# A recurrent-attention and mixture-of-experts kernel: units 0 to 3 and steps 0 to 13 in a written order, weight conversion cut into single operations

## The chip, the cores and the metric

The kernel runs on one core of one Trainium2 chip. Its time is the device time of one execution in microseconds (us), the median of several. A profile of one further execution gives every instruction's start and end on the engines: PE (TensorE, with its weight loads shown apart as PEld), DVE (VectorE), ACT (ScalarE), POOL (GpSimd) and SP (SyncE, which here only issues DMA transfers).

## What is computed

Three layers follow one another. A recurrent attention over 768 tokens for 2 batches of 8 heads of 48, a dense layer of 384 to 2048 to 384 with an exponential unit, and 8 experts of 384 to 1024 to 384, one chosen per token. The dense layer's weights come as 64-bit floats, the others as 32-bit.

```python
for t in range(S):
    kt, vt, rt = (k[:, :, t], v[:, :, t], r[:, :, t])
    cur = np.einsum('bhd,bhe->bhde', u[None] * kt, vt)
    y[:, :, t] = np.einsum('bhd,bhde->bhe', rt, state + cur)
    state = w[None, :, :, None] * state + np.einsum('bhd,bhe->bhde', kt, vt)
...
h = x @ w_in
g = np.where(h > 0.0, h, alpha * (np.exp(np.minimum(h, 0.0)) - 1.0))
return (g @ w_out).astype(np.float32)
...
expert_idx = np.argmax(logits, axis=1)
h = np.maximum(np.einsum('ecd,edf->ecf', disp, w1), 0.0)
y = np.einsum('ecf,efd->ecd', h, w2)
out[i] = gate_w[i] * y[expert_idx[i], pos[i]]
```

## The kernel before, in words

**Units.** The recurrence is cut into 24 units: a unit is 128 tokens of one batch and four heads. `Unit` has these parts: `decay` (DVE, scales `rk`), `bonus` (two products on `tok`, DVE for units 0 to 7, then POOL), `diagonal` (a sum on DVE, then an affine select on POOL that makes `am`), `scores` (PE into the one bank `a`), `mask` (DVE, reads `a`, completes `am`), `decay_kt` (DVE, `kh`), `out` (PE, into the one bank `y`, from `am` and the state `st`), `state` (PE, into bank `u`), `carry` (ACT or DVE, `u` to `st`), `split_y` (ACT, the high part of `y` in `yh`), `split_y_low` (DVE, the low part), and `pack`, DMAs that lay `yh` into `xT`. Units of the same half of the heads (u, u + 2, ...) hand a state on.

**Steps.** The dense layer runs in 48 steps q. A step multiplies one block of 256 tokens (`xT[g]`, four units) with two blocks of 128 columns: `ff_in` (18 matmuls), then `elu_exp`, `elu_min` (ACT), `elu_max` (DVE), `elu_hi` (ACT), `elu_lo` (DVE in steps 0 to 3, then POOL), and `ff_out(q - 2)` (18 matmuls into banks x0 and x1). Every number is carried as a high and a low part, so each product takes three matmuls. Step 0 needs units 0 to 3, step 4 needs units 4 to 7; steps 0 to 3 hold one whole unit each (`whole`), step 4 and 5 none, later steps half a unit each (`half`).

**Weights.** The 64-bit weights come in 16 pieces of 768 KB, n = 0 to 15 (`SEQ`: pieces 0, 1, 2, 4 of `w_in` and 3, 5, 6, 7 of `w_out` serve steps 0 to 5, the other eight serve steps 8 to 13). A piece goes through a load; a copy of a byte of each number (ACT, `b7`); two bit operations (DVE, `b5`, `b7`); a widening to `f64` (ACT); an OR with the rest of the bits (DVE, `f64<-raw`; a 32-bit float now); the high part (ACT, `w<-f64`); and the low part, which is a difference: for pieces 0, 1, 2, 3 and 5 by PE (identity times `f64` less identity times the high part, then a copy by ACT from bank h), for piece 4 on DVE, for the other ten on POOL (line 230).

**Order.** From step 9 on, the program is written under `manual_schedule`: each engine takes its instructions as written. All before that (units 0 to 3, in steps -8 to -1, and steps 0 to 8) is put in order by a scheduler, from the written one. There, weight conversion is called in portions by the table `FILL`, three stages for a pair of pieces at a time. SP and ACT issue DMAs in their own order, so a DMA that waits for a buffer holds up those behind it.

Of the kernel before, what the change touches and what calls it, by code (L numbers as in the profile page):

```python
# [42 lines left out]

FILL = {-6: (0, 1, 0), -5: (0, 1, 0), -4: (0, 1, 0), -3: (0, 1, 0), -2: (0, 1, 0), -1: (0, 1, 0),
        0: (2, 1, 2), 1: (1, 1, 2), 2: (2, 1, 2), 3: (1, 1, 2), 4: (2, 1, 2), 5: (2, 1, 2), 6: (1, 1, 2), 7: (1, 1, 2),
        8: (1, 1, 2), 9: (1, 1, 0)}
LO_V = (4,)
LO_P = (0, 1, 2, 3, 5)
CARRY_P = range(2, 8)
AUTO = 9  # L50
ELO_V = (0, 1, 2, 3)
BONUS_V = range(8)
INIT = (7, 16)
PACKS = (0, 1, 2, 3, 7)


def rwkv_moe_kernel(tc, rkT, tok, wT, ub, rkvT, wu, w_in, w_out, w_gate, w1, w2, out, cap):
# [113 lines left out]
    def load_f64(n, ahead=True):  # L171


        o, i = SEQ[n]
        src = (w_out if o else w_in)[i // 2, i % 2]
        if 0 < n < 3 and ahead:
            raw = first.tile([P, 768, 2], U32, name=f"raw{n}")
        elif n % 3 == 1:
# [6 lines left out]
    words, side = {}, [att]  # L185

    def bits_f64(n, step, ahead=True):

        raw = raw64[n]
        if step == 0:
            words[n] = side[0].tile([P, 192], U32, tag="b7", name="b7", bufs=2)
            byte = raw.rearrange("p n t -> p (n t)").bitcast(I8).rearrange("p (n t) -> p n t", t=8)[:, :, 4]
            nc.scalar.copy(words[n].bitcast(I8), byte)
        elif step == 1:
            top = words[n]
            t = words[n] = side[0].tile([P, 768], U32, tag="f64", name="f64", bufs=2)
# [5 lines left out]
            nc.scalar.activation(out=t.bitcast(I32), in_=top.bitcast(I8), func=AF.Copy, scale=float(1 << 24))  # L204
        else:
            t = words.pop(n)
            nc.vector.scalar_tensor_tensor(out=t, in0=raw[:, :, 0], scalar=5, in1=t,
                                           op0=ALU.logical_shift_right, op1=ALU.bitwise_or)
            del raw64[n]
            o, i = SEQ[n]  # L210
            dst, pool = (wout_t, wpb) if o else (win_t, [wp])
            if i % 2 == 0:
                if o and not wpb:
                    first.release()
                    wpb.append(tc.alloc_tile_pool(name="wpb", bufs=4, side="left", reuse_waits="tile"))
                dst.append(pool[0].tile([P, 2, 1536], F32R, tag="w", name="w"))
            pending.append((n, dst[i // 2], slice(i % 2 * 768, (i % 2 + 1) * 768), t))
            if not ahead:
                return
            if n == 0:  # L220
                load_f64(5)
            elif 3 <= n < 13:
                load_f64(n + 3)

    def split_bits(n, w, o, t):
        nc.scalar.copy(w[:, 0, o], t.bitcast(F32))
        if n in LO_P:
            two_low.append((w, o, t))
            return
        (nc.vector if n in LO_V else nc.gpsimd).tensor_tensor(  # L230
            out=w[:, 1, o], in0=t.bitcast(F32), in1=w[:, 0, o].bitcast(F32), op=ALU.subtract)

    two_low = []

    def low_bits():

        while two_low:
            w, o, t = two_low.pop(0)
            for a, b in ((0, 512), (512, 768)):
                ps = ps_tile(psH, "h")[:, 0:b - a]  # L240
                group(ps, [(ident, t[:, a:b].bitcast(F32))], stop=False)
                group(ps, [(nident, w[:, 0, o.start + a:o.start + b])], start=False)
                nc.scalar.copy(w[:, 1, o.start + a:o.start + b], ps)  # L243

# [26 lines left out]
    class Unit:  # L271
# [95 lines left out]
        def pack(self):  # L367
# [350 lines left out]
    def prep(u, stage):  # L718
# [58 lines left out]
    def whole(q, n):  # L777

        x = units[n]
        prep(n + 1, 0)  # L780
        while pending:
            split_bits(*pending.pop(0))
        x.scores()
        fill(q, 0)
        prep(n + 1, 2)
        ff_in(q, range(2))
        elu_exp(q)
        elu_min(q)
        x.mask()
        x.out()  # L790
        x.state()
        x.split_y()
        low_bits()
        if q >= LAG:
            ff_out(q - LAG)
        fill(q, 1)
        elu_max(q)
        units.pop(n).split_y_low()
        elu_hi(q)
        finish(q)  # L800
        elu_lo(q)
        x.carry()
        prep(n + 1, 3)
        fill(q, 2)

    def half(q, n, first):

        x = units.get(n)
        ff = 0 <= q < NQ
        if first:  # L810
            prep(n + 1, 0)
        elif not ff:
            prep(n + 1, 2)
        while pending:
            split_bits(*pending.pop(0))
        if not first and ff:
            prep(n + 1, 2)
        fill(q, 0)
        if ff:
            ff_in(q, range(2))  # L820
            elu_exp(q)
            elu_min(q)
        if x and first:
            x.scores()
        elif x:
            x.out()
            x.state()
        low_bits()
        if q - LAG >= 0:
# [3 lines left out]
        elif x:  # L833
            x.split_y()
        fill(q, 1)
        if ff:
# [9 lines left out]
        if x and not first:  # L846
            x.carry()
            prep(n + 1, 3)
        fill(q, 2)

    if True:
        load_unit(2)
        load_f64(0)
        load_unit(3)
        load_f64(1)
        load_unit(4)
        load_f64(2)
        load_unit(5)
        load_f64(3)
        load_f64(4)  # L860
        prep(0, 0)
        prep(0, 2)
        prep(0, 3)
        for q in range(-8, 0):
            half(q, 4 + q // 2, q % 2 == 0)
        for q in range(4):
            whole(q, 4 + q)
        for q in range(4, AUTO):
            half(q, 4 + (q + 2) // 2 if q > 5 else NU, q % 2 == 0)
            if INIT[0] <= q < INIT[0] + 6:  # L870
                init_slots(q - INIT[0])
            elif INIT[1] <= q < INIT[1] + 4:
                init_out(q - INIT[1])
    with tc.manual_schedule():
        for q in range(AUTO, 38):
            half(q, 4 + (q + 2) // 2, q % 2 == 0)
            if INIT[0] <= q < INIT[0] + 6:
# [138 lines left out]
    def again():  # L1016
# [14 lines left out]
        wout_t.clear()  # L1031
        conv[:] = [(n, step) for n in range(16) for step in range(3)]
        load_f64(0, False)
        for n, step in list(conv):
            bits_f64(n, step, False)
            if step == 2:
                x = pending.pop()
                nc.scalar.copy(x[1][:, 0, x[2]], x[3].bitcast(F32))
                sub("v", x[1][:, 1, x[2]], x[3].bitcast(F32), x[1][:, 0, x[2]])
                if n < 15:  # L1040
                    load_f64(n + 1, False)
        conv.clear()
        nc.gpsimd.memset(ohc[0], 0.0)
# [106 lines left out]
```

## Time and profile before

| | us |
|---|---|
| median of 3 runs | 467.74 (467.67 to 471.47) |
| the profiled execution's own time | 469.95 |
| its span, first to last instruction | 468.1 |
| PE busy in the span | 436.8 (93%) |
| DVE, ACT, POOL busy | 256.8, 232.3, 149.0 |

The span is what the views below show. The 1.85 us between span and time lie outside the engines' instructions, and the profiled execution was 2.21 us over the median. Mean granted TensorE clock: 0.974 of full speed.

### The profile page before, as it was taken

What the parts mean: (1) busy time and instruction counts of PE and PEld (TensorE: products, weight loads), DVE (VectorE), ACT (ScalarE), POOL (GpSimd) and SP (SyncE); (2) the same over time, 40 slices, a digit from 0 to 9 for tenths busy, and PEclk for the clock granted to TensorE, in tenths of its full rate; (3) what the DMA queues carried; (4) which work ended last, traced back from release to release, by engine and by line L of the source; (5) the groups of instructions that cost most, each with busy time, mean ns of one, the idle gap of its engine ahead of it and who ended that gap; (6) DMA issues with size and microseconds to landing.
All of it is one profiled execution on the core that took longest, in us unless ns stands there. A gap on an engine that the chain in (4) does not pass through costs nothing. (4 is left out here: it accounts for less than half of the span.)

```text
span 468.1 us, 8885 instructions
## 1 busy us (share of the span) xinstructions
PE 436.8 (93%) x3454; PEld 414.8 (89%) x3454; DVE 256.8 (55%) x500; ACT 232.3 (50%) x382; POOL 149.0 (32%) x173
## 2 busy tenths in 40 slices
PE   1959999989999999999999999998999999999992
PEld 1737878979999999999999999998999999999991
DVE  6665677696337484437443424746755655656410
ACT  3362987867334333433444356644456456455410
POOL 4111135668544545434432332423011011011011
PEclk9987999989999999999999999998999999999997
DMA  8866875634724533131300282342766765763001
GB/s 246 263 216 205 249 257 179 211 100 143 261 67 128 192 120 103 46 97 62 110 21 18 69 321 70 101 154 66 247 203 220 236 214 202 252 225 117 27 29 31
DMA packets 27330, 71.14 MB, mean 152 GB/s; under 512 B 4229, under 2 KB 12732, under 8 KB 27280
## 3 DMA queue, kind: packets, MB, share of 16 engines
q1 hardware_dynamic: 24832, 65.06, 42.4%
q0 software_dynamic: 1792, 4.75, 3.0%
q10 hardware_dynamic: 656, 0.69, 0.5%
q8 instruction: 29, 0.48, 0.5%
q14 instruction: 21, 0.17, 0.1%
HBM read 53.89 MB, written 12.46 MB: 142 GB/s over the span
## 5 line engine op out<-in xcount | busy, mean ns | idle before, releaser
L391 PE MATMUL h<-xT,w 128*128 128x256 f32 x864 | 113.4, 285 | 1.1 <-DMA xT<-yh 1.1
L443 PE MATMUL x<-g,w 128*128 128x256 f32 x864 | 114.0, 286 | 0.2 <-ACT w L243 0.2
L443 PEld LDWEIGHTS x<-g,w 128*128 128x128 f32 x864 | 106.1, 191 | 3.9 <-issue 1.0
L391 PEld LDWEIGHTS h<-xT,w 128*128 128x128 f32 x864 | 106.7, 190 | 2.1 <-DMA xT<-yh 1.3
L413 POOL TENSOR_TENSOR g<-e,g 128x512 fp32r<-128x512 f32 x44 | 57.3, 1302 | 106.2 <-ACT g L410 106.2
L607 DVE TENSOR_TENSOR w<-raw,w 128x1536 fp32r<-128x1536 f32 x32 | 57.1, 1784 | 34.3 <-ACT w L606 33.5
L268 PE MATMUL y<-w,ht 128*112 128x384 f32 (+1 forms) x384 | 73.0, 339 | 0.0
L268 PE MATMUL h<-dT,w 128*128 128x240 f32 x576 | 69.8, 275 | 0.0
L268 PEld LDWEIGHTS h<-dT,w 128*128 128x128 f32 x576 | 68.9, 189 | 0.2 <-ACT dT L645 0.2
L406 DVE SCALAR_TENSOR_TENSOR e<-h,e 128x512 f32<-128x512 f32 x48 | 33.0, 686 | 59.3 <-ACT e L402 59.1
L268 PEld LDWEIGHTS y<-w,ht 128*112 128x112 f32 (+1 forms) x384 | 65.2, 181 | 0.2
L398 ACT ACTIVATE e<-h 128x512 f32<-128x512 f32 x48 | 28.6, 597 | 62.3 <-PE h L391 60.7
L707 POOL DMA_INDIRECT out<-o,ds x16 | 15.5, 966 | 121.5 <-ACT o L705 119.1
L606 ACT CAST w<-raw 128x1536 fp32r<-128x1536 f32 x32 | 47.3, 1477 | 0.0
L677 ACT ACTIVATE ht<-h 128x480 fp32r<-128x480 f32 x32 | 18.3, 572 | 57.5 <-PE h L268 57.0
L410 ACT CAST g<-e 128x512 fp32r<-128x512 f32 x48 | 29.8, 621 | 32.1 <-DVE e L406 30.9
L678 DVE SCALAR_TENSOR_TENSOR ht<-h,ht 128x480 fp32r<-128x480 f32 x32 | 21.0, 656 | 32.9 <-ACT ht L677 32.9
L295 POOL TENSOR_SCALAR_AFFINE_SELECT am<-dt 128x512 f32<-128x512 f32 x24 | 17.7, 737 | 45.3 <-PE y L268 24.3
L402 ACT ACTIVATE e<-e 128x512 f32<-128x512 f32 x48 | 30.3, 632 | 1.3
L318 DVE COPY_PREDICATED am<-maskf,a 128x512 f32<-128x512 int32 x24 | 17.8, 740 | 16.7 <-PE a L268 16.6
L268 PE MATMUL a<-rk 48*128 48x128 f32 x192 | 19.7, 325 | 7.1 <-DVE rk L282 6.2
L268 PEld LDWEIGHTS a<-rk 48*128 48x128 f32 x192 | 14.5, 208 | 11.2 <-DVE rk L282 6.2
(137 smaller groups left out, 458.3 us busy)
## 6 DMA issues: line engine op xcount, KB each, us to landing
raw<-w SPq DMA_DIRECT2D x32, 768.0 KB, 5.9
tok<-tok SPq DMA_DIRECT2D x24, 288.0 KB, 3.4
raw<-w_in SPq DMA_DIRECT2D x8, 767.6 KB, 6.8
raw<-w_out SPq DMA_DIRECT2D x8, 767.6 KB, 4.6
rk<-rkT SPq DMA_DIRECT2D x24, 224.0 KB, 3.1
disp<-zrow SPq DMA_DIRECT2D x6, 776.0 KB, 6.0
out<-zrow SPq DMA_DIRECT2D x4, 576.0 KB, 4.2
xT<-yh SPq DMA_DIRECT2D x22, 96.0 KB, 2.3
```

Of the source, the lines that this page charges most:

```text
L268: nc.tensor.matmul(out, x, y, start=start and n == 0, stop=stop and n == len(pairs) - 1, skip_group_check=True)
L391: nc.tensor.matmul(h_ps[:, j], win(d, f, a), x[:, :, d, c], start=n == 0, stop=n == 8)
L398: nc.scalar.activation(out=e, in_=hps[q], func=AF.Exp)
L402: nc.scalar.activation(out=elu[q], in_=elu[q], func=AF.Relu, bias=1.0, scale=-1.0)
L406: nc.vector.scalar_tensor_tensor(out=e, in0=hps.pop(q), scalar=0.0, in1=e, op0=ALU.max, op1=ALU.subtract)
L410: nc.scalar.copy(gt[q][:, 0], elu[q])
L413: eng("v" if q in ELO_V else "p").tensor_tensor(out=gt[q][:, 1], in0=elu.pop(q), in1=gt[q][:, 0].bitcast(F32), op=ALU.subtract)
L443: nc.tensor.matmul(o, wout(f, d, a), gg[:, c, j], start=pr in x2at[g] and j == 0 and n == 0 and d != 1, stop=pr + 1 in x2at[g] and j == 1 ...
L606: nc.scalar.copy(w[:, 0], raw)
L607: low.tensor_tensor(out=w[:, 1], in0=raw, in1=w[:, 0].bitcast(F32), op=ALU.subtract)
L677: nc.scalar.activation(out=ht[:, 0], in_=h_ps, func=AF.Relu)
L678: nc.vector.scalar_tensor_tensor(out=ht[:, 1], in0=h_ps, scalar=0.0, in1=ht[:, 0].bitcast(F32), op0=ALU.max, op1=ALU.subtract)
```

## The change

The whole program up to the experts now stands under `manual_schedule`. Units 0 to 3 (with parts of unit 4) are written out in `first_units`. Weight conversion is cut into single operations with one letter each: R is the load of a piece, K the byte copy, A the two bit operations, L the widening, B the OR, H the high part, W the low part (for pieces 0 to 3 the matmuls of it, whose copy by ACT is V); U is the load of a unit. The table `PLAN` says which stand at which place (a, b, v, w, d, e, f) of which step up to 12. The low parts of pieces 6 to 15 are now on DVE, of 4 and 5 on POOL, of 0 to 3 on PE (through banks x0 and x1 in place of h). `elu_lo` of steps 0 to 3 comes one step later. Loads of pieces and units stand later among the other transfers, the load of piece 0 ahead of those of units 2 and 3; which packing DMAs ACT issues changes (`PACKS`).

```diff
-FILL = {-6: (0, 1, 0), -5: (0, 1, 0), -4: (0, 1, 0), -3: (0, 1, 0), -2: (0, 1, 0), -1: (0, 1, 0),
...
-LO_V = (4,)
-LO_P = (0, 1, 2, 3, 5)
+PLAN = {0: {"b": "B2 R5", "d": "K4 H2", "e": "B3 R6", "f": "H3 U7"},
+        1: {"b": "A4", "v": "W2", "d": "V2 L4 K5", "w": "W3", "e": "B4 R7", "f": "V3 H4 K6 U8"},
...
+for n in range(8, 16):
+    PLAN[n - 3] = {"b": f"B{n} " + (f"R{n + 3} " if n < 13 else "") + (f"A{n + 1}" if n < 15 else ""),
+                   "d": f"H{n} " + (f"L{n + 1} " if n < 15 else "") + (f"K{n + 2}" if n < 14 else ""), "f": f"W{n}"}
+LO_V = range(6, 16)
+LO_P = range(4)
...
-PACKS = (0, 1, 2, 3, 7)
+PACKS = (3, 7)
...
+        elif n in LO_P and side[0] is att:
+            low_bits(op, n)
...
+            hi, lo = place64(n)
+            (nc.vector if n in LO_V or side[0] is not att else nc.gpsimd).tensor_tensor(
+                out=lo, in0=whole64.pop(n).bitcast(F32), in1=hi.bitcast(F32), op=ALU.subtract)
...
+                ps = low_ps[n, a] = ps_tile(psX, tag)[:, 0:b - a]
...
-                (nc.scalar if self.u in PACKS and n % 2 == 0 else nc.sync).dma_start(
+                (nc.scalar if self.u in PACKS and n % 2 else nc.sync).dma_start(
...
+        x[2].scores()
+        x[1].out()
+        x[1].split_y()
+        do("A0 K1 L0")
+        x[1].state()
+        end(1)
+        do("R3")
+        x[1].carry()
+        x[2].mask()
+        begin(3)
+        x[2].decay_kt()
+        middle(3)
+        x[3].scores()
+        x[2].out()
+        x[2].split_y()
+        do("A1 L1 B0 H0")
...
+    with tc.manual_schedule():
+        do("R0 U2 U3 R1")
+        first_units()
         for q in range(4):
             whole(q, 4 + q)
-        for q in range(4, AUTO):
...
+        for q in range(4, 38):
+            step(q)
```

Three places show what the scheduler had made of the order and what is written now. The first is ACT around the carry of unit 2 (`st_f0`) and the high part of unit 2's y (`yh_299` before, `yh_295` now). Before:

```order
L339 COPY st_f0_150<-u_294 48x2x48 x2
L204 ACTIVATE f64_301<-b7_259 128x768
L226 CAST w_322<-f64_279 128x768
L195 COPY b7_374<-raw2_188 128x768
L243 CAST w_322<-h_341 128x512
L243 CAST w_322<-h_345 128x256
L226 CAST w_322<-f64_301 128x768
L204 ACTIVATE f64_426<-b7_374 128x768
L195 COPY b7_376<-raw_194 128x768
L226 CAST w_452<-f64_426 128x768
L195 COPY b7_518<-raw_196 128x768
L360 CAST yh_299<-y_148 112x2x128
```

On the same engine now:

```order
L225 ACTIVATE f64_260<-b7_216 128x768
L350 COPY st_f1_151<-u_262 48x2x48 x2
L371 CAST yh_295<-y_148 112x2x128
L225 ACTIVATE f64_300<-b7_258 128x768
L231 CAST w_303<-f64_260 128x768
L350 COPY st_f0_150<-u_305 48x2x48 x2
```

Before, unit 2's `yh` stood behind ten rows of conversion that come after the carry; now it stands ahead of the widening of piece 1.

The second place is DVE around the mask of unit 9, in steps 8 and 9 (`e<-h` is `elu_max`, `f64<-raw` the OR of a piece). Before:

```order
L406 SCALAR_TENSOR_TENSOR e_994<-h_975,e_994 128x512
L363 TENSOR_TENSOR yh_1024<-y_148,yh_1024 112x2x128
L207 SCALAR_TENSOR_TENSOR f64_1026<-raw_900,f64_1026 128x768
L200 TENSOR_SCALAR b5_1115<-b7_1060 128x192
L202 SCALAR_TENSOR_TENSOR b7_1060<-b7_1060,b5_1115 128x192
L318 COPY_PREDICATED am_968<-maskf_129,a_1084 128x512
L207 SCALAR_TENSOR_TENSOR f64_1114<-raw_952,f64_1114 128x768
```

Now:

```order
L293 TENSOR_TENSOR rk_751<-rk_751,ew_100 112x512
L228 SCALAR_TENSOR_TENSOR f64_974<-raw_814,f64_974 128x768
L219 TENSOR_SCALAR b5_1032<-b7_976 128x192
L221 SCALAR_TENSOR_TENSOR b7_976<-b7_976,b5_1032 128x192
L329 COPY_PREDICATED am_942<-maskf_129,a_1063 128x512
L417 SCALAR_TENSOR_TENSOR e_1054<-h_1035,e_1054 128x512
L236 TENSOR_TENSOR w_1057<-f64_974,w_1057 128x768
```

One OR, one pair of bit operations and one low part now stand in each step, the low part last.

The third place is POOL from step 4 on (line 230 before and line 236 now are low parts of weights, lines 413 and 424 `elu_lo`). Before:

```order
L230 TENSOR_TENSOR w_755<-f64_732,w_755 128x768
L230 TENSOR_TENSOR w_824<-f64_809,w_824 128x768
L413 TENSOR_TENSOR g_815<-e_788,g_815 128x512
L413 TENSOR_TENSOR g_877<-e_853,g_877 128x512
L230 TENSOR_TENSOR w_824<-f64_818,w_824 128x768
L230 TENSOR_TENSOR w_899<-f64_883,w_899 128x768
L230 TENSOR_TENSOR w_951<-f64_888,w_951 128x768
```

Now:

```order
L236 TENSOR_TENSOR w_460<-f64_616,w_460 128x768
L306 AFFINE_SELECT am_689<-dt_687 128x512
L424 TENSOR_TENSOR g_809<-e_782,g_809 128x512
L424 TENSOR_TENSOR g_866<-e_838,g_866 128x512
L299 TENSOR_TENSOR tok_655<-tok_655,u_bc_93 128x192
L300 TENSOR_TENSOR tok_655<-tok_655 128x192
L424 TENSOR_TENSOR g_936<-e_901,g_936 128x512
```

The low parts of weights are gone from POOL behind piece 5.

## Rows read from the trace of the kernel before

**Rows 1.** Four stretches: length, busy us of each engine, granted clock, DMA share, GB/s.

```profile
0.00:42.20 42.20, 26.26 (x150) 19.72 (x150) 26.73 (x77) 17.81 (x38) 8.76 (x26) 0.88 0.71 227
42.20:73.20 31.00, 29.13 (x209) 24.31 (x207) 21.60 (x42) 23.90 (x45) 9.40 (x12) 1.00 0.81 259
73.20:122.40 49.20, 47.13 (x394) 45.09 (x395) 35.16 (x51) 34.36 (x56) 31.77 (x23) 0.97 0.52 169
122.40:468.00 345.60, 334.23 (x2706) 325.69 (x2704) 173.30 (x332) 156.28 (x244) 99.06 (x113) 0.99 0.40 131
```

**Rows 2.** Waits of PE up to 125 us: for whom, total, times, longest.

```profile
PE y L268 <- DVE yh L363: 4.8, 1, 4.8
...
PE y L268 <- DVE am L318: 2.1, 1, 2.1
```

**Rows 3.** Instructions in order of time, first units: start, length, engine, line.

```profile
5.48 0.68 DVE L282 TENSOR_TENSOR rk<-rk,ew 112x512 f32<-112x512 f32 x1
...
21.82 1.10 PE L268 MATMUL y<-am,tok 128*48 128x128 f32 x8
...
34.42 0.36 ACT L360 CAST yh<-y 112x256 fp32r<-112x256 f32 x1
...
38.26 0.42 DVE L363 TENSOR_TENSOR yh<-y,yh 112x256 fp32r<-112x256 f32 x1 [2.73 <-ACT yh L360]
...
42.21 0.98 PE L391 MATMUL h<-xT,w 128*128 128x256 f32 x6
```

**Rows 4.** Groups by line and shape, DVE, 0 to 43 us: busy, mean ns, idle before.

```profile
L282 DVE TENSOR_TENSOR rk<-rk,ew 112x512 f32<-112x512 f32 x8 | 5.8, 730 | 1.0 <-DMA rk<-rkT 1.0
L318 DVE COPY_PREDICATED am<-maskf,a 128x512 f32<-128x512 int32 x6 | 4.4, 727 | 2.4 <-PE a L268 2.4
L207 DVE SCALAR_TENSOR_TENSOR f<-raw,f 128x768 uint32<-128x768 uint32 x3 | 2.9, 955 | 0.7 <-ACT f L204 0.7
...
L288 DVE TENSOR_TENSOR tok<-tok,u_bc 128x192 f32<-128x192 f32 x7 | 2.5, 354 | 0.5 <-DMA u_bc<-ub 0.5
...
L363 DVE TENSOR_TENSOR yh<-y,yh 112x256 fp32r<-112x256 f32 x5 | 2.1, 424 | 7.4 <-ACT yh L360 7.4
...
L200 DVE TENSOR_SCALAR b<-b 128x192 uint32<-128x192 uint32 x5 | 1.3, 257 | 1.1 <-ACT b L195 1.1
```

**Rows 5.** Instructions in order of time, around step 9 and before step 4.

```profile
66.14 1.05 PE L268 MATMUL h<-f,idwg 128*128 128x512 f32 x2
...
73.19 0.95 PE L391 MATMUL h<-xT,w 128*128 128x256 f32 x6 [1.14 <-DMA xT<-yh]
...
97.20 2.67 POOL L230 TENSOR_TENSOR w<-f,w 128x768 fp32r<-128x768 f32 x1 [2.27 <-ACT w L226]
...
103.13 3.79 PE L443 MATMUL x<-g,w 128*128 128x256 f32 x18
```

**Rows 6.** Groups by line and shape, all engines, 0 to 125 us.

```profile
L230 POOL TENSOR_TENSOR w<-f,w 128x768 fp32r<-128x768 f32 x10 | 19.6, 1965 | 9.7 <-ACT w L226 7.5 <-DMA raw<-w_out 2.2
L207 DVE SCALAR_TENSOR_TENSOR f<-raw,f 128x768 uint32<-128x768 uint32 x16 | 17.4, 1086 | 8.4 <-ACT f L204 8.4
...
L413 POOL TENSOR_TENSOR g<-e,g 128x512 fp32r<-128x512 f32 x9 | 12.1, 1340 | 10.0 <-ACT g L410 10.0
...
L200 DVE TENSOR_SCALAR b<-b 128x192 uint32<-128x192 uint32 x16 | 7.7, 483 | 4.2 <-ACT b L195 4.1
L202 DVE SCALAR_TENSOR_TENSOR b<-b,b 128x192 uint32<-128x192 uint32 x16 | 7.6, 476 | 0.4
...
L230 DVE TENSOR_TENSOR w<-f,w 128x768 fp32r<-128x768 f32 x1 | 1.0, 959 | 0.5 <-ACT w L226 0.5
```

**Rows 7.** Instructions in order of time, PE, the `ff_in` of steps 10 and 12.

```profile
106.75 2.31 PE L391 MATMUL h<-xT,w 128*128 128x256 f32 x18
...
117.32 2.31 PE L391 MATMUL h<-xT,w 128*128 128x256 f32 x18
```

**Rows 8.** The loads of weight pieces up to 60 us, from issue to landing.

```profile
DMA to landing us min/median/max: 4.1/6.4/9.8
```

More of the change, by code (lines that the diff above doesn't have):

```diff
@@ L225, in split_bits @@
[L225 to L243, printed above, removed]
+        elif op == "L":
+            t = whole64[n] = side[0].tile([P, 768], U32, tag="f64", name="f64", bufs=2)
+            nc.scalar.activation(out=t.bitcast(I32), in_=words.pop(n).bitcast(I8), func=AF.Copy, scale=float(1 << 24))
+        elif op == "B":
+            t = whole64[n]
+            nc.vector.scalar_tensor_tensor(out=t, in0=raw64.pop(n)[:, :, 0], scalar=5, in1=t,
+                                           op0=ALU.logical_shift_right, op1=ALU.bitwise_or)
+        elif op == "H":
+            nc.scalar.copy(place64(n)[0], whole64[n].bitcast(F32))
+        elif n in LO_P and side[0] is att:
+            low_bits(op, n)
+        else:
+            hi, lo = place64(n)
+            (nc.vector if n in LO_V or side[0] is not att else nc.gpsimd).tensor_tensor(
+                out=lo, in0=whole64.pop(n).bitcast(F32), in1=hi.bitcast(F32), op=ALU.subtract)
@@ new lines, in rwkv_moe_kernel, with low_bits, do @@
+    low_ps = {}
+    def low_bits(op, n):
+        hi, lo = place64(n)
+        for tag, a, b in (("x0", 0, 512), ("x1", 512, 768)):
+            if op == "W":
+                ps = low_ps[n, a] = ps_tile(psX, tag)[:, 0:b - a]
+                group(ps, [(ident, whole64[n][:, a:b].bitcast(F32))], stop=False)
+                group(ps, [(nident, hi[:, a:b])], start=False)
+            else:
+                nc.scalar.copy(lo[:, a:b], low_ps.pop((n, a)))
+    def do(ops):
+        for x in ops.split():
+            bits_f64(x[0], int(x[1:]))
@@ L779, in whole, with late_lo @@
         x = units[n]
+        plan = PLAN[q]
+        x.scores()
+        x.mask()
         prep(n + 1, 0)
[L781 to L784, printed above, removed]
+        late_lo()
+        do(plan.get("a", ""))
+        ff_in(q, range(2))
         prep(n + 1, 2)
-        ff_in(q, range(2))
+        do(plan.get("b", ""))
         elu_exp(q)
         elu_min(q)
-        x.mask()
+        do(plan.get("v", ""))
         x.out()
+        x.split_y()
         x.state()
-        x.split_y()
-        low_bits()
+        do(plan.get("w", ""))
+        do(plan.get("d", ""))
+        units.pop(n).split_y_low()
         if q >= LAG:
             ff_out(q - LAG)
-        fill(q, 1)
+        x.carry()
         elu_max(q)
-        units.pop(n).split_y_low()
+        prep(n + 1, 3)
+        do(plan.get("e", ""))
         elu_hi(q)
         finish(q)
[L801 to L804, printed above, removed]
+        do(plan.get("f", ""))
+    def late_lo():
+        for q in list(elu):
+            if q in gt:
+                elu_lo(q)
     def half(q, n, first):
@@ L809, in half @@
         ff = 0 <= q < NQ
+        plan = PLAN.get(q, {}) if side[0] is att else {}
+        late_lo()
         if first:
             prep(n + 1, 0)
-        elif not ff:
+        else:
             prep(n + 1, 2)
[L814 to L818, printed above, removed]
+        do(plan.get("b", ""))
         if ff:
@@ L848, in half, with first_units, begin, middle @@
             prep(n + 1, 3)
[L849 to L865, printed above, removed]
+        do(plan.get("f", ""))
+    def first_units():
+        x = [None] * 5
+        def begin(n):
+            x[n] = units[n] = Unit(n)
+            x[n].decay()
+        def middle(n):
+            x[n].bonus()
+            x[n].diagonal()
+        def end(n):
+            units.pop(n)
+            x[n].split_y_low()
+        begin(0)
+        middle(0)
+        x[0].scores()
+        begin(1)
+        x[0].mask()
+        middle(1)
+        x[0].decay_kt()
+        x[1].scores()
+        x[0].out()
+        do("K0")
+        x[0].split_y()
+        begin(2)
+        x[1].mask()
+        x[0].state()
+        end(0)
+        do("U4 R2")
+        x[1].decay_kt()
+        x[0].carry()
+        middle(2)
+        x[2].scores()
[14 more added lines that the diff above has]
+        do("A1 L1 B0 H0")
+        x[2].state()
+        end(2)
+        do("U5")
+        x[2].carry()
+        x[3].mask()
+        begin(4)
+        x[3].decay_kt()
+        do("K2 B1")
+        x[3].out()
+        x[3].split_y()
+        do("H1")
+        x[3].state()
+        end(3)
+        do("R4 U6 W0 V0 K3")
+        x[3].carry()
+        middle(4)
+        x[4].decay_kt()
+        do("A2 W1 V1 L2 A3 L3")
@@ L1031, in again @@
         wout_t.clear()
-        conv[:] = [(n, step) for n in range(16) for step in range(3)]
         load_f64(0, False)
[L1034 to L1042, printed above, removed]
+        for n in range(16):
+            do(f"K{n} A{n} L{n} B{n} H{n} W{n}")
+            if n < 15:
+                load_f64(n + 1, False)
         nc.gpsimd.memset(ohc[0], 0.0)
```

83 lines of the change are left out of this document (30 added, 53 removed), and 3 rows, old and new, of the table PLAN.

## The prediction

> **What bounds the kernel now.** I read the stretches first, because one average hides three regimes. PE is the engine that the end hangs on: from 122.4 us to the end it is busy 334.2 of 345.6 us [rows 1], and the order there is the same in both programs, so whatever the change brings must show as an earlier start of that stretch, which is `ff_in` of step 13. Ahead of it there are three stages. In the first, to 42.2 us (the first `ff_in`), PE is busy 26.3 of 42.2 us, much of it at half speed (granted clock 0.88), so it is a chain that bounds, not PE. In the second, steps 0 to 3, PE is busy 29.1 of 31.0 us: nearly bound. In the third, steps 4 to 12, 47.1 of 49.2 us.
>
> Next, who makes PE wait. The longest wait of an order's making is 4.8 us for unit 2's low part on DVE [rows 2]. The time line says why: the last matmuls of unit 2's y end at 22.9 us, but ACT makes the high part of that y only at 34.42 us [rows 3], 11.5 us later. DVE is not what it waited for; ACT had ten conversion rows in front. The second wait, 2.1 us for a mask [rows 2], is in step 9: there low parts on POOL take up to 2.67 us, and 18 matmuls of `ff_out` take 3.79 us [rows 5] where an undisturbed `ff_in` of 18 takes 2.31 us [rows 7]: after its pause PE ran part of them slower (mean granted clock 0.97 in that stage [rows 1]). The undisturbed pace is that of rows 7: 10.57 us for two steps, 5.28 us each.
>
> **Part 1: units 0 to 3 as written.** The number wanted is when the first `ff_in` can start. DVE has the longest list. From the first `decay`, which starts at 5.48 us [rows 3] and moves little, to unit 3's low part, it now holds 5 `decay` and 4 masks at 0.73, 2 ORs at 0.96, 4 low parts at 0.42, 2 bit operations at 0.26, and 19 small ones (bonus, diagonal, `kh`, the second bit operation, the negated identity) at 0.35 [rows 4] (shapes without a row are taken as the 128x192 one): 6.6 + 1.9 + 1.7 + 0.5 + 6.7 = 17.4 us. Without a wait unit 3's low part ends at 22.9 us; before it ended at 38.7 us [rows 3]. Waits come on top. I followed the rows of the new order by hand, with one bank `a` (scores of a unit behind the mask of the one before), one bank `y` (out behind the low part of the one before) and PE at its slow pace (1.10 us for the y matmuls [rows 3]): DVE waits for unit 1's y, for unit 2's y and a little for unit 3's, about 2.5 us in all. So 25.3 us.
>
> Behind it come the packing DMAs: before, 3.5 us from the end of unit 3's low part to the first matmul of `ff_in` [rows 3]. That gives 28.8 us. But PE has its own list: unit 3's state ends at about 26.2 us, then low parts of pieces 0 and 1, then the scores of unit 4. The two fp32 passes of a 512-wide piece take 1.05 us [rows 5], so a piece of 768 about 1.6 us; half-speed doubles part of it, and piece 1's must wait for ACT's copy out of x0. I take 2.2 us each and 0.7 us for scores: 31.3, say **31.5 us in place of 42.2, a gain of 10.7 us**. The floor is 28.5 us (PE's list hidden behind the packing); with both low parts at half speed and 2 us more of waits it is 35 us.
>
> The loads that are moved: piece 0 now goes ahead of units 2 and 3, 768 KB, which at the 227 GB/s of this stage [rows 1] delays unit 2's by 3.5 us at most. By my walk through the new order unit 2's `decay` is due at about 10.8 us and its scores wait for unit 1's mask until about 12.2 us anyway. This costs 0 to 2 us of the chain; I take 0. Later pieces stand behind packing DMAs on SP; the first copies of pieces 2 and 3 are due on ACT at about 23 and 29 us, 8 and 10 us after their loads can be issued, against 6.4 us to land [rows 8]. Nothing is lost while landing stays under 8 us.
>
> **Part 2: steps 0 to 3.** PE was nearly full here, so only work that leaves helps. Before, four pieces (1, 2, 3, 5) had their low parts made by PE in this stage, now two (2 and 3; piece 1 is done earlier and counted above, piece 5 goes to POOL): 2 x 1.6 = 3.2 us off 31.0, so 27.8. On the other side ACT holds eleven rows in step 1, some 8 us, a little more than PE; and step 4 again waits for the packing of unit 7 (1.1 us before [rows 5]), now with less PE work to cover it. I take 29 us, between 27.5 and 32: **a gain of 2 us**.
>
> **Part 3: steps 4 to 12.** The low parts of ten pieces were on POOL, 1.97 us each; now ten (6 to 15) are on DVE at 0.96 [rows 6]: 9.6 us more for DVE. Against this stands what DVE lost beside POOL: its bit operations took 0.483 and 0.476 us in the mean where they take 0.257 and 0.354 alone, the OR 1.086 against 0.955 [rows 4, 6]: 16 x (0.226 + 0.122 + 0.131) = 7.7 us. So DVE's 35.2 us of this stage [rows 1] become about 37, in 46 us: it fits. ACT's list is the old one. With the masks no longer behind stretched bit operations, the 2.1 us wait and the slow matmuls behind it go; what is late next is PE itself, at the pace of rows 7. Seven steps at 5.28 us are 37.0; steps 4 and 5 have no unit but ACT's `keep_half` in the way, 9 us together: 46 us in place of 49.2, **a gain of 3 us**. Bounds: 44.5 (nothing waits in steps 4 and 5), and 52 for the rival below.
>
> **Sum.** 10.7 + 2 + 3 = 15.7 us. A fixed order cannot take another instruction when one is late; for this I take back 2 us, the idle time that PE had in the third stage [rows 1]. Gain 13.7 us, and step 13 at 108.7 us. The profiled execution would take 469.95 - 13.7 = 456.3 us; it was 2.2 us above the median of 467.74, so the median comes to **454 us**. One per cent, 4.7 us, is about what a measurement of this kernel can tell from no change.
>
> **A rule of the skill that speaks against it.** In rows 6 the operations of DVE grow beside POOL, and POOL's low part grows to 2.67 us [rows 5]. The Trainium skill, "SBUF — State Buffer", "Who interferes with whom", says that a DVE instruction with two SBUF inputs and a GpSimd instruction that reads SBUF exclude each other for the whole instruction. The subtraction moved to DVE is such an instruction, so by that rule it gives no relief against what stays on POOL. The first rival below works this out from rows.
>
> **Rivals.**
> (A) *DVE becomes the bound in steps 4 to 12.* POOL keeps `elu_lo`, 1.34 us a step [rows 6], and half of each later unit's bonus. If DVE stands still for each `elu_lo` and half a microsecond more, its step is 37 / 9 = 4.1 us plus 1.8, 5.9 against PE's 5.28: 0.65 x 9 = 6 us. Time 460. For it: DVE is the engine that got work. Against it: POOL's load falls by 8 low parts, 15.7 us, and what was stretched most stood beside the low parts now gone.
> (B) *The change does not do what it says for the first units:* they stay bound by loads and by PE at half speed, so that only about half of part 1 is got and parts 2 and 3 are eaten by waits. Gain 5 us, 463. For it: DMA share 0.71 in the first stage [rows 1]. Against: ACT held unit 2's y for 11.5 us with the data there.
> (C) *Slower: loads of pieces 9 to 15.* Each load now waits on SP for the OR three pieces earlier, and the copy of its bytes stands on ACT a little over one step, 6.3 us, behind it, ahead of the next `elu_exp`. If loads land after 9.8 us [rows 8], ACT stands still 3.5 us for each of 7 pieces, and PE with it: 24 us, 478 us. It decides from 8.3 us on (7 x 2 us eat the 14). Against: the median is 6.4 us in the stretch with the fullest queues, and this stage's DMA share is 0.52 [rows 1].
> (D) *All of it at the floor:* 28.5, 27.5 and 44.5 us, 100.5 for step 13, a gain of 22 us: 446.
>
> **How the numbers follow.** Forecast 0.58, A 0.18, B 0.10, C 0.06, D 0.08. Faster by over 1% (under 463.1): the forecast, A, D and a third of B, 0.87. Slower by over 1%: C, 0.06. Between: 0.07. The range holds the forecast and A and most of D: from 447 to 462; left out are B, C and the end of D.
>
> **What would show it.** In the changed profile: the first `ff_in` near 31.5 us, with unit 2's `yh` on ACT within 1 us of its matmuls; `ff_in` of step 4 near 60.5 and of step 13 near 108.7 us, with full clock from step 0 on; no mask wait in step 9; DVE's bit operations near 0.26 and 0.35 us; SP loads landing before their copy. Part 1 is wrong if PE waits over 2 us for `xT` at step 0 or DVE for loads of units 2 and 3. A shows as PE waits for DVE in steps 4 to 12, C as ACT waits for `raw`. The whole is wrong if something behind step 13 moves, for example the order of the tail's DMAs, which I take as fixed.

## The result, and the profile of the changed kernel

The changed kernel took 456.19 us in the median of four runs (455.42 to 456.84), the kernel before beside it 468.15 us: a ratio of 0.973 (95% interval 0.968 to 0.978), 12.0 us less. The profiled execution of the changed kernel took 456.53 us with a span of 454.8 us, so the spans, which the views show, differ by 13.3 us.

The stretches of the changed kernel, cut where those of before were cut (first `ff_in`, `ff_in` of step 4, of step 13, end), with the same columns:

```profile
0.00:30.70 30.70, 19.84 (x120) 14.63 (x120) 21.95 (x62) 15.38 (x35) 7.00 (x25) 1.00 0.80 238
30.70:60.00 29.30, 27.39 (x227) 23.59 (x225) 25.98 (x48) 23.29 (x44) 10.17 (x8) 1.00 0.77 238
60.00:109.10 49.10, 46.98 (x400) 44.37 (x401) 41.05 (x64) 35.69 (x57) 22.16 (x18) 1.00 0.67 221
109.10:454.80 345.70, 334.15 (x2706) 325.76 (x2704) 176.11 (x337) 157.68 (x246) 100.59 (x115) 0.99 0.40 133
```

Against [rows 1] the first stretch lost 11.5 us, the second 1.7, the third 0.1 and the last nothing. So most of what the change is worth lies ahead of the first `ff_in`; nine steps in a new order, with ten subtractions moved to another engine, are worth nothing in sum.

The waits of PE up to 125 us (for whom, total, times, longest):

```profile
PE a L279 <- DVE rk L293: 7.4, 2, 6.2
PE x L279 <- ACT w L250: 1.7, 1, 1.7
...
PE x L454 <- ACT half L437: 1.3, 1, 1.3
...
PE x L454 <- POOL w L236: 0.7, 1, 0.7
PE x L454 <- DVE w L236: 0.6, 2, 0.4
```

The 4.8 us for unit 2's low part and the 2.1 us for the mask of step 9 [rows 2] are gone. New are four small waits of `ff_out` (x, line 454), for three writers, and 1.7 us in the first units, where PE's low part of piece 1 waits for ACT to copy that of piece 0 out of x0. The 6.2 us is the start of the program, before the first data.

The chain that bounded the first stretch, instructions in order of time:

```profile
12.07 0.69 DVE L293 TENSOR_TENSOR rk<-rk,ew 112x512 f32<-112x512 f32 x1 [1.13 <-DMA rk<-rkT]
...
20.20 1.10 PE L279 MATMUL y<-am,tok 128*48 128x128 f32 x8
...
21.34 0.37 ACT L371 CAST yh<-y 112x256 fp32r<-112x256 f32 x1 [2.24 <-PE y L279]
...
25.69 0.42 DVE L374 TENSOR_TENSOR yh<-y,yh 112x256 fp32r<-112x256 f32 x1 [1.18 <-ACT yh L371]
...
28.27 1.13 PE L279 MATMUL x<-f,idwg 128*128 128x512 f32 x2 [1.73 <-ACT w L250]
...
30.75 2.42 PE L402 MATMUL h<-xT,w 128*128 128x256 f32 x18
```

Unit 2's y ends at 21.30 and its high part starts 0.04 us later, where 11.5 us lay between them before [rows 3]. The order has turned round: ACT now waits for PE. Unit 3's low part ends at 26.1 us (38.7 before) and the first `ff_in` starts at 30.75, straight behind PE's other work and without a wait in front of it. The first row is a cost of the moved load: DVE waits 1.13 us for the data of unit 2, which now come behind piece 0.

The starts of `ff_in` of steps 4, 9, 10, 11 and 13:

```profile
60.01 2.51 PE L402 MATMUL h<-xT,w 128*128 128x256 f32 x18 [1.24 <-DMA xT<-yh]
...
84.79 2.32 PE L402 MATMUL h<-xT,w 128*128 128x256 f32 x18
90.67 2.32 PE L402 MATMUL h<-xT,w 128*128 128x256 f32 x18
97.11 2.32 PE L402 MATMUL h<-xT,w 128*128 128x256 f32 x18
...
109.13 2.31 PE L402 MATMUL h<-xT,w 128*128 128x256 f32 x18
```

Those of steps 9 and 13 in the kernel before (step 10 is in [rows 7]):

```profile
97.14 2.37 PE L391 MATMUL h<-xT,w 128*128 128x256 f32 x18
...
122.41 0.76 PE L391 MATMUL h<-xT,w 128*128 128x256 f32 x5
```

Step 9 took 9.61 us before and takes 5.88 now: 3.73 gained. Steps 10 to 12 took 15.66 together and now take 18.46: 2.80 lost. Steps 4 to 8 take 0.83 more, but PE is busy in all of them in both kernels; before, part of step 4's `ff_out` stood ahead of the cut. That is the 0.1 us of the third stage: not an unmoved stage, but a gain of which most is given back.

### The profile page after: what moved, and what is told of

Its sections match the earlier page's. It is cut to its first block, busy times and chain, and to the rows that moved or that the text cites. A ratio compares the mean times of both kernels' runs of the same rounds, so it can differ in the third digit from the quotient of the medians.

```text
span 454.8 us, 8861 instructions
## 1 busy us (share of the span) xinstructions
PE 428.4 (94%) x3448; PEld 408.4 (90%) x3448; DVE 265.1 (58%) x509; ACT 232.0 (51%) x380; POOL 139.9 (31%) x165
## 5 line engine op out<-in xcount | busy, mean ns | idle before, releaser
L454 PEld LDWEIGHTS x<-g,w 128*128 128x128 f32 x864 | 104.5, 188 | 6.0 <-ACT half L437 1.5
L424 POOL TENSOR_TENSOR g<-e,g 128x512 fp32r<-128x512 f32 x44 | 58.9, 1338 | 124.4 <-ACT g L421 124.4
```

The lines of the kernel that those rows point to most:

```text
L424: eng("v" if q in ELO_V else "p").tensor_tensor(out=gt[q][:, 1], in0=elu.pop(q), in1=gt[q][:, 0].bitcast(F32), op=ALU.subtract)
L454: nc.tensor.matmul(o, wout(f, d, a), gg[:, c, j], start=pr in x2at[g] and j == 0 and n == 0 and d != 1, stop=pr + 1 in x2at[g] and j == 1 ...
```

## The experiments

Each ratio is to the kernel before in runs on the same chip; the changed kernel's is 0.973 (0.968 to 0.978).

**Unit 2's y behind the conversion again.** In `first_units`:

```diff
         x[2].out()
-        x[2].split_y()
         do("A1 L1 B0 H0")
         x[2].state()
+        x[2].carry()
+        do("K2")
+        x[2].split_y()
         end(2)
         do("U5")
-        x[2].carry()
...
-        do("K2 B1")
+        do("B1")
```

> The changed kernel with one thing moved back: on ACT the high part of unit 2's y stands behind the widening of piece 1, the high part of piece 0 and the byte copy of piece 2 (2.6 us of work), as conversion stood ahead of it before the change. If ACT's order in the first units is what made the first ff_in late (my part 1), the high part comes 2.5 to 3.5 us later and the first ff_in starts 2 to 3.5 us later, at 33 to 34 us in place of 30.7; the time is 458.5 to 460. Rival: PE's own list and the packing hide it (both ended together at 30.7 us); then the first ff_in moves by less than 1 us and the time stays at 456 to 457.

Measured: 458.81 us (457.31 to 460.95), ratio 0.981 (0.977 to 0.985). ACT in order of time, and PE's wait for it, in this kernel:

```profile
24.76 0.86 ACT L215 COPY b<-raw 128x768 int8<-128x768 int8 x1
25.65 0.37 ACT L371 CAST yh<-y 112x256 fp32r<-112x256 f32 x1
```

```profile
PE y L279 <- DVE yh L374: 2.3, 1, 2.3
```

Four ACT rows in front of that one `yh`, against ten in the kernel before: unit 2's y ends at 22.48 us and waits 3.2 us for ACT, and PE waits 2.3 us behind it where it waited 4.8 [rows 2]. The first `ff_in` comes 4.1 us later (34.81) and step 13 3.1 us later (112.22). So who stands in front on ACT does set the first `ff_in`: three rows of conversion and the carry bring back 4.1 of the 11.5 us. The wait names DVE, as it did before, and again DVE was only passing it on.

**The scheduler back for units 0 to 3 only**, the steps as written:

```diff
-    with tc.manual_schedule():
+    if True:
         do("R0 U2 U3 R1")
         first_units()
+    with tc.manual_schedule():
         for q in range(4):
```

> The changed program with the scheduler back for units 0 to 3 alone (first_units stays as written but its instructions may be moved), steps 0 on in the written order. The run with the scheduler back for steps 0 to 8 kept the whole gain, so if the gain is the written order of the first units, this run must lose it: first ff_in at 36 us or later, time 461 to 467. Rival: what counts is that the conversion is cut into single operations placed between the units, which the scheduler gets here too; then the first ff_in stays at 30 to 33 us and the time at 455 to 458.

Measured: 460.07 us (459.13 to 460.75), ratio 0.981 (0.976 to 0.986). The first `ff_in`, and unit 3's high part on ACT:

```profile
33.45 4.18 PE L402 MATMUL h<-xT,w 128*128 128x256 f32 x18 [3.23 <-DMA xT<-yh]
```

```profile
29.89 0.36 ACT L371 CAST yh<-y 112x256 fp32r<-112x256 f32 x1
```

Neither theory holds whole. The scheduler, given the new written order and single operations as its input, keeps unit 2's y in time (ACT takes it at 21.08 us, 0.1 us behind its matmuls), and 8.7 us of gain stay (468.76 to 460.07). It puts conversion ahead of unit 3's y, which ends at 26.4 us and is taken at 29.89 (25.29 in the changed kernel), and PE then waits 3.2 us for the packing of it. So the fixed order of these units is worth about 4 us (step 13 at 113.12). The rest stays when the scheduler gets the new program; which part of the new program brings it is not shown.

**The scheduler back for steps 0 to 8**, `first_units` as written:

```diff
         first_units()
+    if True:
         for q in range(4):
             whole(q, 4 + q)
-        for q in range(4, 38):
+        for q in range(4, 9):
+            step(q)
+    with tc.manual_schedule():
+        for q in range(9, 38):
             step(q)
```

> The changed program with the scheduler back for steps 0 to 8 only; units 0 to 3 stay in the written order, the single operations of the conversion stand where the plan has them, but the scheduler may move them. If the gain sits in the first units (11.5 of 13.3 us of span), the first ff_in stays at 30.5 to 32 us and the time is 456 to 461. Rival: fixing the order of the steps matters as much; then steps 0 to 8 stretch and the time is 463 or more.

Measured: 455.75 us (453.49 to 456.45), ratio 0.974 (0.970 to 0.977); step 13 at 109.36 us. Two of its rows of PE, the `ff_in` of steps 10 and 13:

```profile
93.70 2.32 PE L402 MATMUL h<-xT,w 128*128 128x256 f32 x18
...
109.36 2.32 PE L402 MATMUL h<-xT,w 128*128 128x256 f32 x18
```

In sum nothing is lost; the time is a little under the first forecast. Inside the run much moves. The first `ff_in` comes at 35.39 us, not at 30.5 to 32: the scheduler puts work of unit 4 and of the low parts ahead of it. PE then waits 2.4 us for a high part, and step 9 starts 3.0 us later than in the changed kernel (87.82). But steps 10 to 12, written as before, take 15.66 us without a wait, where the changed kernel takes 18.46. DVE's low parts in them start within 0.2 us of where they start in the changed kernel. So the written order brings PE to step 9 earlier by 3.0 us, and 2.8 of them are lost in the waits of steps 10 to 12.

**The low parts of pieces 6 to 15 back on POOL:**

```diff
-LO_V = range(6, 16)
+LO_V = ()
```

> The changed kernel with the low parts of pieces 6 to 15 back on POOL, all else as written. My part 3 said that beside POOL's low parts DVE's bit operations are stretched and that the move to DVE pays for itself: then steps 4 to 12 take 52 us or more in place of 49.1 and the time is 459 to 463. Rival, the exclusion of DVE and POOL: it does not matter on which of the two engines the subtraction stands, since each blocks the other for as long; then steps 4 to 12 take 48.5 to 50.5 us and the time is 455.5 to 458.

Measured: 464.83 us (463.14 to 466.40), ratio 0.994 (0.990 to 0.997), step 13 at 118.92 us. PE's waits, then POOL and PE in order of time in step 11:

```profile
PE x L454 <- POOL w L236: 6.4, 4, 2.8
PE h L402 <- POOL w L236: 1.5, 1, 1.5
```

```profile
101.72 3.30 POOL L236 TENSOR_TENSOR w<-f,w 128x768 fp32r<-128x768 f32 x1
...
105.08 2.18 PE L402 MATMUL h<-xT,w 128*128 128x256 f32 x16 [1.53 <-POOL w L236]
```

In the written order the move is needed: without it most of the gain is gone, more than either forecast said. PE waits directly for POOL, 7.9 us (0.7 of them stand in the changed kernel too), where a low part takes 1.8 to 3.3 us behind other work of POOL's queue. That is a reason I had not given. Mine was that DVE's other operations are stretched; they are (in steps 4 to 12 a pair of bit operations took 1.48 us here and 1.17 with the move, a `decay` 1.43 and 1.16), but in these steps no wait of PE names DVE.

**The same move alone, in the kernel before:**

```diff
-LO_V = (4,)
+LO_V = (4, *range(6, 16))
```

> The kernel before with one part of the change alone: the low parts of pieces 6 to 15 on DVE in place of POOL; order by the scheduler as before. If that part by itself is worth my part 3, the slow step 9 goes (9.6 us to about 6) and the time is 463 to 465.5. Rival: the move matters only in the written order, where POOL's low parts stand in line; the scheduler had put them where they cost little, then 466.5 to 469.

Measured: 469.58 us (467.29 to 472.91), ratio 1.001 (0.999 to 1.003). Its DVE groups up to 130 us, and PE's `ff_in` of step 4, which the packing now splits:

```profile
L207 DVE SCALAR_TENSOR_TENSOR f<-raw,f 128x768 uint32<-128x768 uint32 x16 | 15.2, 953 | 3.9 <-ACT f L204 3.9
...
L202 DVE SCALAR_TENSOR_TENSOR b<-b,b 128x192 uint32<-128x192 uint32 x16 | 6.8, 425 | 0.3
L200 DVE TENSOR_SCALAR b<-b 128x192 uint32<-128x192 uint32 x16 | 5.1, 322 | 1.9 <-ACT b L195 1.9
```

```profile
74.19 0.95 PE L391 MATMUL h<-xT,w 128*128 128x256 f32 x6 [0.59 <-DMA xT<-yh]
79.38 2.93 PE L391 MATMUL h<-xT,w 128*128 128x256 f32 x12 [3.77 <-DMA xT<-yh]
```

The time is that of the kernel before, as the rival has it. But the relief is real: 0.322, 0.425 and 0.953 us in place of 0.483, 0.476 and 1.086 [rows 6], 5.5 us over 16 pieces, and step 9 takes 5.88 us, as in the changed kernel. The scheduler, whose order this edit also moves, has steps 0 to 3 later by up to 3 us and then PE waiting 4.4 us for `xT` in step 4. The 3.7 us of step 9 are lost ahead of it. (The profiled execution was the longest of the ten, 472.91 us, so its losses are at the upper end.)

**`elu_lo` of steps 4 to 12 on DVE too:**

```diff
-ELO_V = (0, 1, 2, 3)
+ELO_V = range(13)
```

> The changed kernel with elu_lo of steps 4 to 12 on DVE as well, so that POOL keeps only the affine selects and the bonus of the later units in steps 4 to 12. If DVE's operations are long there because POOL's two-input operations exclude them, the first bit operation falls from a mean of 0.54 us to 0.35 or less and the second from 0.59 to 0.42 or less, DVE's busy time in steps 4 to 12 stays at 41 us or falls although it gets nine subtractions of 0.69 us (6.2 us), and the time stays within 455 to 457.5. Rival: the operations are long for another reason (DVE's own queue); then DVE's busy time rises by 6 us to 47 of 49, PE waits for it, and the time is 459 or more.

Measured: 461.12 us (460.63 to 464.29), ratio 0.987 (0.983 to 0.991), step 13 at 114.34 us.

```profile
PE x L454 <- DVE w L236: 3.3, 2, 2.0
...
PE y L279 <- DVE am L329: 1.0, 1, 1.0
```

```profile
L424 DVE TENSOR_TENSOR g<-e,g 128x512 fp32r<-128x512 f32 x8 | 5.5, 692 | 7.4 <-ACT g L421 7.2
```

The time is the rival's, but not its reason. `elu_lo` brings 5.5 us to DVE in that stage, yet DVE's busy time is 42.65 us there, 1.6 more than in the changed kernel: most other operations got shorter, a `decay` from 1.16 to 0.69 us, a pair of bit operations from 1.17 to 0.93. So `elu_lo` on POOL did stretch them. DVE is not full, 42.65 of 55.30 us. But it takes its rows as written and stands 7.2 us in front of `elu_lo` until ACT has made the high part (`g`, line 421), with low parts of weights behind; PE then waits 4.3 us for DVE, and 2.3 us for `half`. Over all 16 pieces the bit operations stay at 0.48 and 0.52 us in the mean, so `elu_lo` is not the only thing on POOL that stretches them; what is left there in steps 4 to 12 are `bonus` and the affine select.

**`keep_half` ahead of the conversion in steps 5 and 9** (`finish` ahead of the widening and byte copy):

```diff
-        do(plan.get("d", ""))
+        d = plan.get("d", "").split()
+        early = 1 if q in (5, 9) else len(d)
+        do(" ".join(d[:early]))
...
+        if q in (5, 9) and early < 9:
+            finish(q)
+            do(" ".join(d[early:]))
...
-        finish(q)
+        if q not in (5, 9):
+            finish(q)
```

> The changed kernel with ACT's copy of banks x0 and x1 (keep_half, steps 5 and 9) moved ahead of the widening and the byte copy of that step. In the changed kernel ff_out of step 10 waits 1.26 us for that copy, which stood behind an ACT row that waited for DVE and one that waited for a load. If that order is what steps 9 and 10 lose, the wait goes and the time falls by 1 to 1.5 us, to 454.7 to 455.2. Rival: the next wait (low parts of pieces 13 and 14 on DVE, 0.4 and 0.3 us) grows by what is gained, since the widening of piece 13 now comes later; then no change, 455.8 to 456.8.

Measured: 455.16 us (453.71 to 456.38), ratio 0.971 (0.966 to 0.975). The time is inside the first forecast, though not clear of the changed kernel's; the trace shows the effect. The wait for `half` is gone and step 10 takes 5.10 us (92.11 to 97.21), not 6.44. The profiled step 13 is only 0.5 us earlier (108.67), since step 4 came 1.4 us later, with 1.5 us of wait for `xT`.

**Piece 0's load behind unit 2's**, and its byte copy behind unit 0's y:

```diff
+        x[0].split_y()
         do("K0")
-        x[0].split_y()
...
-        do("R0 U2 U3 R1")
+        do("U2 R0 U3 R1")
```

> The changed kernel with the load of piece 0 behind that of unit 2 (as before the change) and its byte copy behind the high part of unit 0's y on ACT. In the changed kernel DVE waits 1.13 us for unit 2's rk and ACT 1.64 us for piece 0. If the moved load costs part of the chain, the decay of unit 2 starts at about 11 us in place of 12.07 and the first ff_in 0.5 to 1.1 us earlier, time 455 to 455.7. Rival, my part 1 (the load costs nothing, because the chain waits elsewhere): first ff_in within 0.3 us of 30.7, time 456 to 456.5.

Measured: 454.82 us (453.10 to 456.85), ratio 0.970 (0.965 to 0.974). Unit 2's `decay` starts at 10.47 us, in place of 12.07, and waits for nothing; the first `ff_in` starts at 29.72, step 13 at 107.48 us. The load that I had priced at nothing, with the byte copy behind it, cost 1.0 us of the chain. Step 10 takes 5.66 us here with `keep_half` where it was, since ACT's byte copy does not wait for its load as it did in the profile of the changed kernel (0.68 us).

**Both of these edits together:**

> Both of the two edits before (keep_half early; the load of piece 0 behind unit 2's). If both are on the path they add: 453.8 to 455. Rival: whatever is gained in the first units is lost at the wait for xT of step 4 or in the low parts; then 455.5 to 456.5.

Measured: 453.08 us (452.20 to 454.31), ratio 0.966 (0.962 to 0.970), step 13 at 106.94 us. The two add up, to a little under the forecast.

**Both, and the bit operations ahead of the next unit's bonus and diagonal:**

```diff
-        2: {"b": "W4 A5 A6", "d": "L5 L6", "e": "B5 R8", "f": "H5 U9"},
+        2: {"b": "A5 A6 W4", "d": "L5 L6", "e": "B5 R8", "f": "H5 U9"},
...
+        do(plan.get("b", ""))
         prep(n + 1, 2)
-        do(plan.get("b", ""))
...
+        do("A0")
         middle(2)
...
-        do("A0 K1 L0")
+        do("K1 L0")
```

The lines of the two edits before are left out here. The ORs that stand in the same place (b) move ahead with the bit operations.

> The changed kernel with both edits of the run before (keep_half early, load of piece 0 later), and the two bit operations of a piece ahead of the diagonal on DVE wherever they stood behind it, so that they no longer start together with POOL's affine select. In the changed kernel the second bit operation took 0.80 us in place of 0.36 beside each affine select that began with it. If affine select and the bit operation exclude each other, the mean of the second bit operation falls from 0.59 to 0.48 us or less and DVE's busy time up to step 13 falls by 1.5 us or more; the time falls by 0 to 1 us against the run with both edits, since PE is the bound there: 452 to 453.5. Rival: the affine select meets the next DVE operation with two inputs instead, and DVE's busy time stays within 1 us.

Measured: 452.85 us (451.64 to 453.48), ratio 0.966 (0.963 to 0.969). Its DVE groups up to 112 us:

```profile
L228 DVE SCALAR_TENSOR_TENSOR f<-raw,f 128x768 uint32<-128x768 uint32 x16 | 15.6, 977 | 0.2 <-ACT f L225 0.2
...
L219 DVE TENSOR_SCALAR b<-b 128x192 uint32<-128x192 uint32 x16 | 7.8, 487 | 1.2 <-ACT b L215 1.1
L221 DVE SCALAR_TENSOR_TENSOR b<-b,b 128x192 uint32<-128x192 uint32 x16 | 7.5, 466 | 0.6
```

Without this last edit they were 1.068, 0.537 and 0.522 us: 3.2 us of DVE over 16 pieces. In the trace PE's waits for DVE's low part are gone, steps 10 to 12 take 15.66 us, as in the kernel before (16.56 without this edit), and step 13 starts at 105.22 us, 1.7 earlier; 0.8 of that come ahead of step 5. In the time the two kernels can't be told apart. Both lie about 3 us under the changed kernel (not run beside it; their ranges of times don't meet its range, while the intervals of the ratios just touch).

## Why the prediction came out

It said 454 us; 456.19 was measured, inside a range of 447 to 462, and the place of the gain was right. For the profiled execution it said 456.3 us, and that took 456.53. The miss in the median is the step between the two: the profiled execution before was 2.2 us above the median, that of the changed kernel 0.3. That the sum came so close is in part luck: part 3 was 2.9 us too high, part 2 0.3 too high, part 1 0.8 too low, and the 2 us taken back for a fixed order, for which there was no row but PE's idle time, covered the difference.

**Part 1** forecast the first `ff_in` at 31.5 us: 30.75. Unit 3's low part was forecast to end at 25.3: 26.1. The list of DVE rows was right; the waits were others than named. DVE did not wait for unit 1's y, but 1.13 us for unit 2's load, 0.79 and 1.18 us for the y of units 2 and 3, and 0.5 us for a select on POOL. On PE's list two entries were off against each other: unit 3's state ended at 24.9 us, not 26.2, but the low parts of pieces 0 and 1 took until 30.17, 5.3 us and not 4.4. Each was cheaper than taken (piece 0's took 1.8 us, 24.70 to 26.54, against 2.2), but 1.73 us of wait for ACT's copy lay between them; ACT issued two packing DMAs from 26.15 to 27.59 and began the copy at 27.63. The moved load cost 1.0 us where I took nothing. The granted clock was 1.00 in the whole stretch, where it was 0.88 [rows 1]. I had read 0.88 as half speed for much of the stretch; in the trace before the clock was 1.00 in each ten us up to 30 and 0.56 from 30 to 40 us. Rival B (half of part 1) is out.

**Part 2** forecast 29 us for steps 0 to 3: 29.3. The wait of step 4 for `xT` stayed, 1.24 us, as assumed.

**Part 3** is the term that was mis-sized: a gain of 3 us against 0.1, which the 2 us allowance for a fixed order mostly hid. Its start was right: the mask wait and the slow matmuls went, and step 9 fell from 9.61 to 5.88 us. Steps 4 and 5 were right (8.71 us, forecast 9). The pace of the seven steps behind them was not: 40.4 us, forecast 37.0. 2.8 of the difference lie in steps 10 to 12; the other 0.6 are work, since steps 7 and 9 hold a `state` (5.9 us each) that the steps of rows 7 lack. Only in the last experiment they took 37.6 (105.22 - 67.60). What failed is the step ahead of it, that DVE would be relieved by 7.7 us and be busy about 37: it was busy 41.05 us. DVE groups of steps 4 to 12, before and then now:

```profile
L207 DVE SCALAR_TENSOR_TENSOR f<-raw,f 128x768 uint32<-128x768 uint32 x8 | 9.7, 1218 | 4.2 <-ACT f L204 4.2
...
L200 DVE TENSOR_SCALAR b<-b 128x192 uint32<-128x192 uint32 x7 | 5.2, 749 | 2.3 <-ACT b L195 2.2
L202 DVE SCALAR_TENSOR_TENSOR b<-b,b 128x192 uint32<-128x192 uint32 x7 | 4.4, 630 | 0.2
```

```profile
L228 DVE SCALAR_TENSOR_TENSOR f<-raw,f 128x768 uint32<-128x768 uint32 x9 | 9.6, 1065 | 0.0
L236 DVE TENSOR_TENSOR w<-f,w 128x768 fp32r<-128x768 f32 x9 | 9.4, 1046 | 0.1
...
L221 DVE SCALAR_TENSOR_TENSOR b<-b,b 128x192 uint32<-128x192 uint32 x8 | 4.7, 593 | 0.3
...
L219 DVE TENSOR_SCALAR b<-b 128x192 uint32<-128x192 uint32 x8 | 4.6, 578 | 0.0
```

A pair of bit operations fell from 1.38 to 1.17 us and an OR from 1.22 to 1.07: 8 x 0.21 + 9 x 0.15 = 3.0 us of relief, not 7.7. The low parts brought 9.4 us, and one pair and one OR more fall into this stage, 2.2 us. (Lengths of rows overlap a little, so they don't add up to the busy time.) The overlaps show why the relief is small; DVE and POOL in order of time:

```profile
15.17 0.63 POOL L306 TENSOR_SCALAR_AFFINE_SELECT am<-dt 128x512 f32<-128x512 f32 x1 [3.75 <-DVE b L219]
15.21 0.80 DVE L221 SCALAR_TENSOR_TENSOR b<-b,b 128x192 uint32<-128x192 uint32 x1
...
88.20 0.95 DVE L228 SCALAR_TENSOR_TENSOR f<-raw,f 128x768 uint32<-128x768 uint32 x1
88.27 2.03 POOL L424 TENSOR_TENSOR g<-e,g 128x512 fp32r<-128x512 f32 x1 [4.44 <-ACT g L421]
89.07 1.35 DVE L219 TENSOR_SCALAR b<-b 128x192 uint32<-128x192 uint32 x1
```

`elu_lo` (L424), asked for while DVE runs the OR, ends 1.15 us after the OR; the bit operation that DVE begins next ends 0.12 us after `elu_lo`, 1.35 us long in place of 0.26. The Trainium skill, "SBUF — State Buffer", "Who interferes with whom", describes this: whoever issues first has the shared pair of ports for the whole instruction and the other stands still. The trace agrees for the OR, which has two inputs, and `elu_lo`. The bit operation at 89.07 has one input, for which the section has contention only in some modes of DVE; which mode it ran in no run shows. My weighing took the stretch as belonging to the low parts on POOL; it belongs to whatever POOL begins beside DVE, and the written order has `elu_lo`, `bonus` or the affine select beginning there in many steps. The experiment with `elu_lo` on DVE bears this out for `elu_lo`; in the scheduler's old order, moving the low parts alone gave 5.5 us of the 7.7.

PE lost the gain of step 9 again in steps 10 to 12. ACT and PE in order of time, step 10:

```profile
91.16 0.85 ACT L225 ACTIVATE f<-b 128x768 int32<-128x768 int8 x1 [1.09 <-DVE b L221]
92.69 0.88 ACT L215 COPY b<-raw 128x768 int8<-128x768 int8 x1 [0.68 <-DMA raw<-w_out]
...
94.26 0.58 ACT L437 COPY half<-x 128x512 f32<-128x512 f32 x1
...
94.89 2.37 PE L454 MATMUL x<-g,w 128*128 128x256 f32 x18 [1.26 <-ACT half L437]
```

`keep_half`, which frees the banks of x, stands behind a widening that waits for the stretched bit operation and a byte copy that waits for its load. With `keep_half` ahead of them step 10 is back at 5.10 us; with the bit operations moved as well, steps 11 and 12 are back at 5.47 and 5.09. These two experiments account for the 2.8 us. It is not the price of a fixed order as such: steps 9 to 12 were in a written order before the change too. But there the last OR ended at 107.3 us, as step 10 began, and DVE was busy 9.11 of the 15.66 us of steps 10 to 12; now two ORs and two pairs of bit operations stand in these steps, with a third OR at their end (108.72), and DVE is busy 15.62 of 18.46.

**The rivals.** A (DVE the bound) did not happen at its size of 6 us: PE waited 0.6 us for DVE's low parts and 0.2 for a mask in those steps. But its mechanism is what ate DVE's relief, and by way of ACT it has a share in the 1.26 us for `half`. Its edge is near in steps 10 to 12: DVE was busy 14.61 of 15.66 us there with the scheduler back for steps 0 to 8. C (loads land late, slower) is out at its size: ACT waited 0.7 us for a load in steps 4 to 12, ahead of `keep_half` in step 10. D was not reached. The tail was fixed as assumed: 345.7 us from step 13 to the end in both traces.

**Open.** How much of the 8.7 us that stay with the scheduler on units 0 to 3 comes from cutting conversion into single operations, and how much from where they are written, was not separated. Which POOL operation stretches which DVE operation is read from overlaps; only `elu_lo`, and the low parts, were taken away by themselves.

## What to carry to other kernels

A wait names the last link; look at what the engine before it had in front in its queue, and put the row that others wait for ahead of those that nobody waits for yet. In a written order this holds for short rows that free a bank as well, which are easily left behind work that waits for a transfer. Before counting a relief from moving work off an engine, look at what stays there and beside what it will begin: a stretch follows the overlap, not the operation that was moved. And look at what the moved operation itself waits for: on an engine that takes its rows as written, everything behind it waits too.

## What was not expected of the hardware

The eight y matmuls of a unit took 1.09 to 1.10 us up to 20.20 us and 0.65 us from 23.26 us on, with a granted clock of 1.00 in both stretches of the changed kernel. In the kernel before they still took 1.10 us at 36.72 and 39.99 us, behind the 4.8 us pause [rows 2]; the granted clock of its stretch from 22.9 to 42.2 us was 0.73. With unit 2's y put late by experiment they took 1.10 us at 27.66, behind a wait of 2.3 us. So slow matmuls were seen behind PE's waits in all three. But with piece 0's load later they took 1.10 us at 22.90 too, with no wait in the 5.9 us before. What sets the pace there stays open; a granted clock of 1.00 did not show it.

An affine select on POOL, whose input is the 4 sums a row of `dt`, took 0.63 us at 15.17, and a bit operation, 0.36 us long elsewhere, that began 0.04 us behind it took 0.80. `elu_lo` itself grew, from 1.340 us in the mean [rows 6] to 1.516, when the long low parts left its engine, probably since it now meets more of DVE's work; that was not tested.
